# Mamba-2 scan with a cosine-gated feed-forward: B and C of seven pairs of sequences loaded in 32-token blocks and transposed by VectorE

## The chip, the cores and the metric

The kernel runs on one core of a Trainium2 chip. The metric is the device time of one execution in microseconds (us). A profiled execution has a span that is a little shorter than the timed one (377.9 us against 379.95 us for the same run), since the span leaves out what lies before the first and after the last instruction. Times inside the kernel are given from the span's start.

## The reference

Two blocks follow each other. The first is a selective state-space scan over `x` (4 sequences, 8 heads, 768 tokens, 32 channels) with a decay `a` per token and head, and `B` and `C` with a state of 16 per token and head. With `cum` the running sum of `log a` inside a chunk, each chunk computes

```
CB      = C_i . B_j                       (over the 16 of the state)
y_intra = (CB * exp(cum_i - cum_j), j <= i) x
y_inter = (C_i . state) * exp(cum_i)
state   = exp(cum_last) * state + sum_j B_j x_j exp(cum_last - cum_j)
y       = y_intra + y_inter
```

The result is brought to 3072 rows (sequence and token) of 256 (head and channel). The second block is `h = y w_in` (256 to 2048), `g = h * cos(h)`, `out = g w_out` (2048 to 256). All is float32.

## The kernel before

The tokens are cut into six chunks of 128 (`NC = 6`), each with four sequences (`b` = 0 to 3). Sequences go in two pairs, `u = 0` and `u = 1`, so there are twelve pairs (chunk, pair). The feed-forward is cut into 16 pieces of 128 of its 2048 columns per chunk (`NF = 16`), and the whole kernel is one loop over 96 such steps `n` plus two (`LAG = 2`). Chunk `c` owns the steps 16c to 16c + 15. The order is written out by hand (`tc.manual_schedule()`): every engine executes its instructions in the order of the program, and a small table, `plan`, says at which steps the scan of chunk c is worked on beside the feed-forward of chunk c - 1.

A step of the feed-forward has a chain over four engines. TensorE multiplies `y` by a piece of `w_in` into a PSUM bank `hp` (L519). ScalarE takes the integer number of turns `k` (L523), VectorE the remainder `w` (L525), ScalarE its sine (L530), VectorE the product `gT` of `hp` and the cosine (L535), GpSimd four differences `gd` for a seven-product form of the second matrix product (L560 to L563). TensorE multiplies them by `w_out` two steps later into `o` (L616; L578 in the first chunk). There are two `hp` banks, so `hp` of step n + 2 has to wait for `gT` of step n.

The scan of a pair takes four stations. Decays (`lam`, L345) come from running products on VectorE. At the step before the pair's turn, `reaches` (L336) makes the running products of `a` along the tokens, on VectorE. At its turn, `turn2` brings B and C from "token on the partition" to "head and state on the partition": four transposes of 128x128 on TensorE through PSUM (`tp`, L406), then `bT` (a copy, L409) and `cT` (two scaled copies, L412) on ScalarE, and `rT = tp * reach` (L414) on VectorE. One step later `intra2` multiplies them (`g`, L423), and `masked` (L436) applies the decays on VectorE. At the end of the pair, or of both pairs of a chunk, `finish2` computes `y` (L450, L457), copies it to `yT`, forms the new sums `s_ps` (L478, which read `x` and the scaled B) and carries the state.

In chunks 2 to 5 the first pair turns at step 16(c - 1) + 7, the second at 16(c - 1) + 11, and both finish at 16(c - 1) + 14. Chunk 1 differs: its first pair turns at step 11 and finishes at 14, its second turns at step 18 and finishes at step 21.

All loads and most stores are issued by SyncE (SP), whose queue is in program order too. A transfer that has to wait, for a buffer or for its data, holds up all behind it. Transfers also take turns on eight semaphores, so each waits for the transfer eight places before it to land. `load` (L119) brings a chunk's B and C (tile `bc`) and x (tile `xr`), with a token on each partition; a load of B for four sequences has 4096 rows of 64 bytes. Chunk c + 2 is loaded at step 16c. These tiles come from a pool with three buffers. `load_a` (L127, `arow`) and `load_along` (L137) fetch the decays for the next chunk, `along` with its 8 heads spread over 128 partitions.

The lines below fix the places of the work, chunk by chunk: the step at which a chunk's plan starts, its pairs' turns, the halves of the decays, and its end.

```
late = [((0,), {0: 11}, [...], 14),
        ((1,), {1: NF + 2}, [...], NF + 5)]
at_once = (0, 1), {0: 7, 1: 11}, 14
```

Of the kernel before, what the change touches and what calls it, by code (L numbers as in the profile page):

```python
# [8 lines left out]
FP32 = mybir.dt.float32  # L9
# [16 lines left out]
def kernel(  # L26
# [29 lines left out]
    nc = tc.nc  # L56
    V, ACT, G, PE = nc.vector, nc.scalar, nc.gpsimd, nc.tensor

    NB, H, S, D = x.shape
    N = B.shape[-1]  # L60
    P = 128
    NC = S // P
    DM, DF = moe_w_in.shape
    KT = DM // P
    NF = DF // P
# [5 lines left out]
    W = P // 2  # L71

    const = ctx.enter_context(tc.tile_pool(name="const", bufs=1))
    loads = ctx.enter_context(tc.tile_pool(name="loads", bufs=3))
    rows = ctx.enter_context(tc.tile_pool(name="rows", bufs=NB))
    scan = ctx.enter_context(tc.tile_pool(name="scan", bufs=2))
    states = ctx.enter_context(tc.tile_pool(name="states", bufs=3))
# [11 lines left out]
    def pair(name):  # L89

        return psum.tile([P, 2, 4 * P], FP32, tag="scan", bufs=2, name=name)


    raw, arow, along = {}, {}, {}
    ones = const.tile([P, P], FP32, name="ones")
    V.memset(ones, 1.0)

# [10 lines left out]
    def load(c, seqs=(0, NB)):  # L108

        if c >= NC:  # L110
            return
        if c not in raw:
            raw[c] = (loads.tile([P, 2, NB * H, N], FP32, tag="bc", name="bc"),
                      loads.tile([P, NB, H, D], FP32, tag="xr", name="xr"))
        bc, xr = raw[c]
        xr = xr.rearrange("p b h d -> p (b h) d")
        rs = slice(seqs[0] * H, seqs[1] * H)
        for dst, src in ((bc[:, 0, rs], B), (bc[:, 1, rs], C), (xr[:, rs], x)):
            nc.sync.dma_start(out=dst, in_=src[seqs[0]:seqs[1], :, c * P:(c + 1) * P, :]  # L119
                              .rearrange("b h s n -> s (b h) n"))  # L120

    def load_a(c, seqs=range(NB)):
        if c >= NC:
            return
        for b in seqs:
            arow[c, b] = t = rows.tile([P, H, P], FP32, tag="arow", name="arow")
            nc.sync.dma_start(  # L127
                out=t, in_=a_cut[b, :, c * P:(c + 1) * P].unsqueeze(0).to_broadcast([P, H, P]))

    def load_along(c, seqs=range(NB)):  # L130

        if c >= NC:
            return
        if c not in along:
            along[c] = rows.tile([P, NB, P], FP32, tag="along", bufs=2, name="along")
        for b in seqs:
            nc.sync.dma_start(  # L137
                out=along[c][:, b], in_=a_all[b, :, c * P:(c + 1) * P].unsqueeze(1)
                .to_broadcast([H, N, P]))
# [20 lines left out]
    def fetch(which, i, eng=nc.sync):  # L160
        src = (moe_w_in[:, i * WC:(i + 1) * WC].rearrange("(k p) f -> p k f", p=P)
               if which == "in" else
               moe_w_out[i * WF * P:(i + 1) * WF * P, :].rearrange("(f p) m -> p f m", p=P))
        if src.dtype == FP32:
            eng.dma_start(out=kept(which, i), in_=src)
            return
        words[which, i] = t = conv.tile([P, 2 * WC, 2], U32, tag="words", bufs=8, name="words")
        eng.dma_start(  # L168
            out=t.rearrange("p (k f) w -> p k (f w)", k=src.shape[1]), in_=src.bitcast(U32))
# [49 lines left out]
    for b in range(NB):  # L219
# [4 lines left out]
        out=a_in, in_=a.rearrange("(u b) h (c p) -> (b h c) u p", u=NU, p=P))  # L224
# [4 lines left out]
    ident = const.tile([P, P], FP32, name="ident")  # L229
# [59 lines left out]
    def heads(b):  # L289
        return slice(b * H, (b + 1) * H)  # L290
# [106 lines left out]

    def turn2(c, u):  # L400
        bc = raw[c][0]

        tp = pair("tp")[:, 0].rearrange("p (s k i) -> p s k i", s=2, k=2)
        for s in range(2):
            for k in range(2):
                PE.transpose(tp[:, s, k],  # L406
                             bc[:, k, heads(2 * u + s)].rearrange("p h n -> p (h n)"), ident)
        bT = scan.tile([P, 2, P], FP32, tag="bT2", bufs=1, name="bT2")
        ACT.copy(out=bT, in_=tp[:, :, 0])  # L409
        cT = scan.tile([P, 2, 2, P], FP32, tag="cT2", bufs=1, name="cT2")  # L410
        for t in range(2):
            ACT.activation(cT[:, :, t], tp[:, :, 1], AF.Copy, scale=slot[:, t:t + 1])  # L412
        rT = scan.tile([P, 2, P], FP32, tag="rT", name="rT")
        V.tensor_tensor(out=rT, in0=tp[:, :, 1], in1=reach[c, u], op=ALU.mult)  # L414
        part[c, u] = [bT, cT, rT]
# [93 lines left out]
    def first(n):  # L509
        c, f = divmod(n, NF)  # L510
        hp[n] = bank([P, TB], "hp", "h")

        u, j = turn_of(n)
        to_ = hp[n].rearrange("p (e t s i) -> p e t s i", e=2, t=2, s=2)
        y = yT[c].rearrange("p k (u s t i) -> p k u t s i", u=2, s=2, t=2)
        for e in range(2):
            fs = slice((2 * j + e) * P, (2 * j + e + 1) * P)
            for k in range(KT):
                PE.matmul(to_[:, e], lhsT=w_in[:, k, fs], rhs=y[:, k, u],  # L519
                          start=(k == 0), stop=(k == KT - 1), skip_group_check=True)  # L520

        k = ffn.tile([P, TB], I32, tag="k", name="k")
        ACT.activation(k, hp[n], AF.Copy, bias=0.25, scale=INV_2PI)  # L523
        turns[n] = w = ffn.tile([P, TB], FP32, tag="w", name="w")
        V.scalar_tensor_tensor(out=w, in0=hp[n], scalar=INV_2PI, in1=k,  # L525
                               op0=ALU.mult, op1=ALU.subtract)

    def gate(n):
        cos = turns[n]
        ACT.activation(cos, cos, AF.Sin, bias=quarter, scale=TWO_PI)  # L530
# [165 lines left out]
    for dst, src in ((a_cut, cut), (a_all, la)):  # L696
        nc.sync.dma_start(
            out=dst.rearrange("(u b) h (c p) -> (b h c) u p", u=NU, p=P), in_=src)
# [27 lines left out]
    def first_scan():  # L726

        finish(3, "o")
        for u in range(2):
            sums[u] = pair("s_ps")[:, :, 0:2 * D]  # L730
            for t in range(2):
                sum_up(0, 2 * u + t, sums[u][:, t])

    def chunk1(b):
        load(1, (b, b + 1))
        load_along(1, (b,))
        load_a(1, (b,))

    def rest_of_loads():
        for w in (("out", 2), 0, ("in", 4), ("out", 3), ("in", 5), ("out", 4), 1,  # L740
                  ("in", 6), ("out", 5), ("in", 7), 2, ("out", 6), ("out", 7), 3):
            chunk1(w) if isinstance(w, int) else fetch(*w)
        load(2)

    def pairs(n):

        return [(c, u) for c, at, _, turn_at, _, _ in plan for u in turn_at
                if at + turn_at[u] == n]
# [4 lines left out]
    def halved(c, b, t):  # L753
        decays(c, b, t)
        if t == 1:
            load_a(c + 1, (b,))

    def ends(n):
        return [(c, us) for c, at, us, _, _, end in plan if at + end == n]

    rest_of_loads()
    for n in range(NC * NF + LAG):
        c, f = divmod(n, NF)
        if n < NC * NF:
            if f == 0 and c > 0:
                load(c + 2)
            first(n)
            if n == 0:
                first_scan()
            for at in pairs(n):  # L770
                turn2(*at)
            rests = [rest] if n == 0 else []
            if n + 1 in piece:
                rests.append(grade(*piece[n + 1], later=True))
            gate(n)
            for rest in rests:
                if rest:
                    rest()
            if n in piece and n > 1:
                join(*piece[n])  # L780

            behind = [lambda at=at: halved(*at) for at in halves_at(n)]
            behind = [lambda at=(c, 2 * u + 1): masked(*at) for c, u in pairs(n - 2)] + behind
            if n not in piece and behind:
                behind.pop(0)()
            gated(n)
            if n < 2:
                join(*piece[n])
            for do in (*behind, *unsummed):
                do()  # L790
            unsummed.clear()
            if n in (1, 2):
                carry(0, n - 1, sums[n - 1])
        for i, js in differ_at.get(n, ()):
            differ_w(i, js)
        if n >= LAG:
            second(n - LAG)
        for c, u in pairs(n - 1):
            intra2(c, u)
            masked(c, 2 * u)  # L800
        for c, us in ends(n):
            finish2(c, us)
            if 1 in us:
                raw.pop(c)
        for c, u in pairs(n + 1):
            for b in (2 * u, 2 * u + 1):
                reaches(c, b)
                load_along(c + 1, (b,))


# [28 lines left out]
```

## Time and profile before

| what | value |
|---|---|
| time, median of three runs (lowest, highest) | 380.73 us (380.5, 380.94) |
| span of the profiled execution | 377.9 us |
| TensorE busy (matmul) | 372.2 us, 98% |
| VectorE busy | 274.4 us, 73% |
| GpSimd busy | 214.3 us, 57% |
| ScalarE busy | 177.1 us, 47% |
| DMA, mean over the span | 80 GB/s, packets 39.6% of 16 engines' time on the main queue |
| TensorE's four transposes per pair (L406) | 40 instructions for ten pairs, 273 ns listed for each |

In the profile, PE is TensorE's matmul, PEld its weight load, DVE is VectorE, ACT ScalarE, POOL GpSimd, and SPq the queue of SyncE. A listed duration of a matmul covers its whole way through the array, and matmuls overlap; what one costs is read from the distance between starts. A float32 matmul shows as two records, a transpose as one. The chain of waits follows the work that ended last back in time; what is on it sets the span.

### The profile page before, as it was taken

How to read it: one execution, taken by the hardware profiler on the slowest of the kernel's cores; microseconds unless marked ns; L12 is line 12 of the kernel's file. 1: busy time of each engine (PE TensorE's matmuls, PEld its weight loads, DVE VectorE, ACT ScalarE, POOL GpSimd, SP SyncE). 2: the span in 40 equal slices, each digit the busy share in tenths (PEclk: the TensorE clock that was granted, in tenths of full speed). 3: DMA queues.
4: the chain of work that ended last, by engine and by line, in shares of the span. 5: the costliest groups of instructions: out<-in, count | busy, mean ns of one | idle time of the engine just before them, and what ended most of it. 6: DMA issues, size and time to landing. Idle time of an engine off the chain costs nothing.

```text
span 377.9 us, 7680 instructions
## 1 busy us (share of the span) xinstructions
PE 372.2 (98%) x2980; PEld 329.6 (87%) x2980; DVE 274.4 (73%) x422; ACT 177.1 (47%) x312; POOL 214.3 (57%) x330
## 2 busy tenths in 40 slices
PE   8999999999999999999999999999999999999996
PEld 2578888889989899998999998899998989999995
DVE  8879999899688747966747985756886762454543
ACT  3887756444435434444434354424444533543442
POOL 6767565579865437673544683443685343454551
PEclk9999999999999999999999999999999999999999
DMA  6989979979230971420681340100010000010011
GB/s 82 234 255 293 255 206 131 182 98 175 78 102 26 148 63 57 135 76 2 82 73 57 83 122 7 42 2 2 1 30 3 10 19 2 0 29 0 2 28 28
DMA packets 106370, 30.41 MB, mean 80 GB/s; under 512 B 75520, under 2 KB 102240, under 8 KB 106336
## 3 DMA queue, kind: packets, MB, share of 16 engines
q1 hardware_dynamic: 106176, 29.81, 39.6%
q8 instruction: 23, 0.38, 0.5%
q10 hardware_dynamic: 160, 0.13, 0.1%
q14 instruction: 11, 0.09, 0.1%
HBM read 26.59 MB, written 3.34 MB: 79 GB/s over the span
## 4 chain that ended last, share of the span: by engine, by line
PE 92%; SPq 3%; DMA 1%; ACT 1%; issue 0%; DVE 0%; POOL 0%; POOLq 0%
PE hp L519 43%; PE o L616 33%; PE o L578 7%; PE g L423 3%; SPq L119 3%; PE y L457 3%; DMA words<-in_moe_w_out_dram 1%; PE y L450 1%; PE tp L406 1%; PE o L661 1%; PE s_ps L478 0%; ACT mag L193 0%; POOL w_out L217 0%; SPq L168 0%; DVE mag L209 0%
## 5 line engine op out<-in xcount | busy, mean ns | idle before, releaser
L519 PE MATMUL hp<-yT,w_in 128*128 128x256 f32 x768 | 183.8, 382 | 0.4 <-POOL w_in L217 0.3
L519 PEld LDWEIGHTS hp<-yT,w_in 128*128 128x128 f32 x768 | 139.4, 190 | 21.2 <-issue 2.9
L560 POOL TENSOR_TENSOR gd<-gT 128x256 f32<-128x256 f32 x79 | 59.8, 757 | 103.6 <-DVE gT L535 79.2
L530 ACT ACTIVATE w<-w,quarter 128x512 f32<-128x512 f32 x96 | 69.3, 722 | 79.3 <-DVE w L525 79.3
L525 DVE SCALAR_TENSOR_TENSOR w<-hp,k 128x512 f32<-128x512 f32 x96 | 65.7, 684 | 54.5 <-ACT k L523 54.3
L523 ACT ACTIVATE k<-hp 128x512 int32<-128x512 f32 x96 | 57.1, 595 | 95.7 <-PE hp L519 95.5
L535 DVE TENSOR_TENSOR gT<-hp,w 128x512 f32<-128x512 f32 x96 | 65.1, 678 | 32.3 <-ACT w L530 27.1
L616 PE MATMUL o<-words,gd 128*128 128x128 f32 x474 | 65.8, 275 | 0.0
L616 PEld LDWEIGHTS o<-words,gd 128*128 128x128 f32 x474 | 59.3, 192 | 0.0
L345 DVE TENSOR_TENSOR_SCAN lam<-arow,unit 128x512 f32<-128x512 f32 x40 | 56.3, 1406 | 0.0
L563 POOL TENSOR_TENSOR gd<-gT,gd 128x128 f32<-128x128 f32 x79 | 47.3, 599 | 6.2
L616 PEld LDWEIGHTS o<-w_out,gT 128*128 128x128 f32 x316 | 46.9, 191 | 3.6
L616 PE MATMUL o<-w_out,gT 128*128 128x128 f32 x316 | 48.0, 274 | 0.0
L562 POOL TENSOR_TENSOR gd<-gT,gd 128x128 f32<-128x128 f32 x79 | 42.4, 537 | 6.2
L578 PE MATMUL o<-w_out,gT 128*128 128x256 f32 x128 | 30.3, 380 | 0.4 <-POOL w_out L217 0.4
L616 PE MATMUL o<-words,gT 128*128 128x128 f32 x158 | 30.6, 275 | 0.0
L616 PE MATMUL o<-w_out,gd 128*128 128x128 f32 x158 | 30.6, 275 | 0.0
L578 PEld LDWEIGHTS o<-w_out,gT 128*128 128x128 f32 x128 | 24.2, 190 | 4.0 <-POOL w_out L217 0.8
L436 DVE TENSOR_TENSOR m<-g,lam 128x512 f32<-128x512 f32 x40 | 25.5, 679 | 0.0
L616 PEld LDWEIGHTS o<-words,gT 128*128 128x128 f32 x158 | 24.0, 192 | 0.0
L616 PEld LDWEIGHTS o<-w_out,gd 128*128 128x128 f32 x158 | 24.0, 192 | 0.0
L633 DVE TENSOR_TENSOR sum<-ps,sum 128x256 f32<-128x256 f32 (+1 forms) x27 | 16.7, 645 | 0.6
(91 smaller groups left out, 280.7 us busy)
## 6 DMA issues: line engine op xcount, KB each, us to landing
arow<-a_cut SPq DMA_DIRECT2D x20, 512.0 KB, 4.1
words<-in_moe_w_in_dram SPq DMA_DIRECT2D x8, 512.0 KB, 6.3
words<-in_moe_w_out_dram SPq DMA_DIRECT2D x8, 512.0 KB, 8.4
out_dram<-sum SPq DMA_DIRECT2D x18, 128.0 KB, 2.5
xr<-in_x_dram SPq DMA_DIRECT2D x4, 512.0 KB
along<-a_all SPq DMA_DIRECT2D x20, 64.0 KB
xr<-in_x_dram SPq DMA_DIRECT2D x8, 128.0 KB
bc<-in_B_dram SPq DMA_DIRECT2D x4, 256.0 KB, 5.0
```

The lines of the kernel that those rows point to most:

```text
L345: V.tensor_tensor_scan(out=lam[c, b][:, hs].rearrange("p h i -> p (h i)"), data0=rows_.rearrange("p h i -> p (h i)"), data1=unit.rearrange ...
L436: V.tensor_tensor(out=of[0], in0=g[q][:, :, s * 2 * P:(s + 1) * 2 * P], in1=of[1], op=ALU.mult)
L519: PE.matmul(to_[:, e], lhsT=w_in[:, k, fs], rhs=y[:, k, u], start=(k == 0), stop=(k == KT - 1), skip_group_check=True)
L523: ACT.activation(k, hp[n], AF.Copy, bias=0.25, scale=INV_2PI)
L525: V.scalar_tensor_tensor(out=w, in0=hp[n], scalar=INV_2PI, in1=k, op0=ALU.mult, op1=ALU.subtract)
L530: ACT.activation(cos, cos, AF.Sin, bias=quarter, scale=TWO_PI)
L535: V.tensor_tensor(out=gT[n], in0=hp.pop(n), in1=cos, op=ALU.mult)
L560: G.tensor_tensor(out=d[:, 0:2], in0=g[:, 1:2].to_broadcast([P, 2, P]), in1=g[:, 3::-3], op=ALU.subtract)
L562: G.tensor_tensor(out=d[:, 2], in0=g[:, 0], in1=d[:, 0], op=ALU.subtract)
L563: G.tensor_tensor(out=d[:, 3], in0=g[:, 2], in1=d[:, 2], op=ALU.subtract)
L578: PE.matmul(o[c, u][:, t], lhsT=g[:, 2 * e + t], rhs=w_out[:, 2 * j + e], start=(j == e == t == 0), stop=(j == NJ - 1 and e == 1), skip_gr ...
L616: PE.matmul(at[q], lhsT=a_[q], rhs=w[q], start=(j == 0 and q in starts), stop=(j == NJ - 1), skip_group_check=True)
```

## The change

For the pairs from chunk 2's second on (seven of twelve), B and C are fetched a second way: in blocks of 32 tokens, so that each partition holds, for one of four heads and one of 32 tokens, the 16 values of the state. A transpose of 32x32 squares on VectorE then gives the layout that four TensorE transposes gave. The aim is to take these transposes, and the copy `bT` behind them, off TensorE and ScalarE.

Per pair this needs 32 transfers (2 sequences, B and C, 4 blocks of tokens, 2 sets of heads) of 128 rows of 64 bytes each. They are issued by SP, four at the end of each of eight steps that start at step 16(c - 1) - 9 + 8u: steps 15 to 22 for chunk 2's second pair, 23 to 30 and 31 to 38 for the pairs of chunk 3, and so on. VectorE's two transposes stand behind `reaches`, at the end of the step before the pair's turn, that is at steps 26, 38, 42, 54, 58, 70 and 74. The block tile takes two buffers, the transposed tile one, which `bT` of the other pairs shares. To make room, the tiles `bc` and `xr` have two buffers instead of three. B is still loaded by tokens for the sums of the state; C of chunks 3, 4 and 5 no longer is.

```diff
-    loads = ctx.enter_context(tc.tile_pool(name="loads", bufs=3))
+    loads = ctx.enter_context(tc.tile_pool(name="loads", bufs=2))
...
-        for dst, src in ((bc[:, 0, rs], B), (bc[:, 1, rs], C), (xr[:, rs], x)):
+        for dst, src in ((bc[:, 0, rs], B), (bc[:, 1, rs], C), (xr[:, rs], x))[::2 if c > 2 else 1]:
             nc.sync.dma_start(out=dst, in_=src[seqs[0]:seqs[1], :, c * P:(c + 1) * P, :]
                               .rearrange("b h s n -> s (b h) n"))
+
+    def by_blocks(c, u):
+        return (c, u) >= (2, 1)
+
+    def load_blocks(c, u):
...
+        blocks[c, u] = to_ = loads.tile([P, 2, 2, 4, 2, N], FP32, tag="blocks", name="blocks")
+        for s in range(2):
+            for k, src in enumerate((B, C)):
+                of = src[2 * u + s, :, c * P:(c + 1) * P].rearrange(
+                    "(q h) (m t) n -> m h q t n", h=2, t=32)
+                for m in range(4):
+                    for h in range(2):
+                        nc.sync.dma_start(out=to_[:, k, s, m, h], in_=of[m, h])
+                        yield
...
+    def turn_blocks(c, u):
+        turned[c, u] = t = scan.tile([P, 2, 2, P], FP32, tag="turned", bufs=1, name="turned")
+        for k in range(2):
+            V.transpose(out=t[:, k].rearrange("p s i -> p (s i)"),
+                        in_=blocks[c, u][:, k].rearrange("p s m h n -> p (s m h n)"))
+        del blocks[c, u]
+
     def turn2(c, u):
         bc = raw[c][0]
...
+        if by_blocks(c, u):
+            tp = turned.pop((c, u)).rearrange("p k s i -> p s k i")
+            bT = tp[:, :, 0]
+        else:
...
+    block_loads = {NF * (c - 1) - 9 + 8 * u: (c, u) for c in range(2, NC) for u in range(2)
+                   if by_blocks(c, u)}
...
             for b in (2 * u, 2 * u + 1):
                 reaches(c, b)
                 load_along(c + 1, (b,))
+            if by_blocks(c, u):
+                turn_blocks(c, u)
+        for at, (c, u) in block_loads.items():
+            if at == n:
+                loading = load_blocks(c, u)
+            if at <= n < at + 8:
+                for _ in range(4):
+                    next(loading)
```

More of the change, by code (lines that the diff above doesn't have):

```diff
@@ L91, in pair @@
         return psum.tile([P, 2, 4 * P], FP32, tag="scan", bufs=2, name=name)
-    raw, arow, along = {}, {}, {}
+    raw, arow, along, blocks = {}, {}, {}, {}
     ones = const.tile([P, P], FP32, name="ones")
@@ L395, in finish @@
         ACT.copy(out=yT[0][:, :, b * P:(b + 1) * P], in_=y[:, 0:2])
+    turned = {}
+    def turn_blocks(c, u):
[4 more added lines that the diff above has]
+        del blocks[c, u]
     def turn2(c, u):
         bc = raw[c][0]
[L403 to L409, printed above, removed]
+        if by_blocks(c, u):
+            tp = turned.pop((c, u)).rearrange("p k s i -> p s k i")
+            bT = tp[:, :, 0]
+        else:
+            tp = pair("tp")[:, 0].rearrange("p (s k i) -> p s k i", s=2, k=2)
+            for s in range(2):
+                for k in range(2):
+                    PE.transpose(tp[:, s, k],
+                                 bc[:, k, heads(2 * u + s)].rearrange("p h n -> p (h n)"), ident)
+            bT = scan.tile([P, 2, 2, P], FP32, tag="turned", bufs=1, name="bT2")[:, 0]
+            ACT.copy(out=bT, in_=tp[:, :, 0])
         cT = scan.tile([P, 2, 2, P], FP32, tag="cT2", bufs=1, name="cT2")
```

## The prediction

> **What bounds the kernel now.** First the page's busy shares and the chain of waits, to see which engine sets the end.
>
> ```profile
> PE 372.2 (98%) x2980; PEld 329.6 (87%) x2980; DVE 274.4 (73%) x422; ACT 177.1 (47%) x312; POOL 214.3 (57%) x330
> ...
> PE 92%; SPq 3%; DMA 1%; ACT 1%; issue 0%; DVE 0%; POOL 0%; POOLq 0%
> ```
>
> TensorE does. From about 25 us on its matmuls follow each other without a gap, so an instruction taken off TensorE shortens the span by its issue time, and a wait put into it lengthens the span by as much. Next the chain in order of time, around one group of four transposes (columns: start, length, what).
>
> ```profile
> 159.44 1.73 PE hp L519 x8
> 161.16 1.56 PE o L616 x14
> 162.73 1.73 PE hp L519 x8
> 164.89 1.56 PE o L616 x14
> ```
>
> Without transposes `o` starts 1.72 us after `hp`; with them 2.16. Four transposes cost TensorE 0.44 us, not four times the 273 ns that one is listed with: they are pipelined.
>
> Then the queue of SyncE, which issues all loads. First the timeline of SP at the start of chunk 1, where chunk 3 is loaded, and the durations of two kinds of transfer from their tiles' views (min/median/max, ns):
>
> ```profile
> 78.81 0.52 SPq L119 DMA_DIRECT2D bc<-in_B_dram  x1
> 79.78 3.07 SPq L119 DMA_DIRECT2D bc<-in_C_dram  x1
> 82.96 3.08 SPq L119 DMA_DIRECT2D xr<-in_x_dram  x1
> 86.14 4.04 SPq L586 DMA_DIRECT2D out_dram<-ob  x2
> 90.27 0.55 SPq L127 DMA_DIRECT2D arow<-a_cut  x1
> 90.91 2.21 SPq L586 DMA_DIRECT2D out_dram<-ob  x2
> 93.18 1.29 SPq L137 DMA_DIRECT2D along<-a_all  x2
> ```
> ```profile
> L137 SPq DMA_DIRECT2D along<-a_all x20: 577/619/812, 26.2 to 242.9; - x20
> L127 SPq DMA_DIRECT2D arow<-a_cut x20: 360/367/2727, 27.1 to 223.4; - x20
> ```
>
> The reader is to see that a transfer holds SP for 0.4 to 0.65 us however small it is, and that the transfer behind a 4096-row load waits some 3 us more. Last the timelines of TensorE and VectorE at the first pair that changes (chunk 2, second pair, step 27), and the chain two steps on:
>
> ```profile
> 99.22 0.41 PE L478 MATMUL s_ps<-xr,sc 128*32 128x64 f32 x16
> ```
> ```profile
> 121.73 0.73 DVE L336 TENSOR_TENSOR_SCAN reach<-along,ones 128x128 f32<-128x128 f32 x2
> 122.38 0.66 DVE L525 SCALAR_TENSOR_TENSOR w<-hp,k 128x512 f32<-128x512 f32 x1
> 122.96 0.41 DVE L414 TENSOR_TENSOR rT<-tp,reach 128x256 f32<-128x256 f32 x1
> 123.29 1.21 DVE L345 TENSOR_TENSOR_SCAN lam<-arow,unit 128x512 f32<-128x512 f32 x1
> 124.42 0.66 DVE L535 TENSOR_TENSOR gT<-hp,w 128x512 f32<-128x512 f32 x1
> ```
> ```profile
> 126.07 1.92 PE hp L519 x8
> ```
>
> The `s_ps` line is the last read of chunk 1's `xr`, at 99.6 us. The last line is `hp` of step 29, which needs the PSUM bank that step 27's `gT` (ended 125.1) sets free: 1.0 us of slack.
>
> **What the Trainium skill says.** "Vector Engine (DVE) Microarchitecture Reference", section 3.8, has the 32x32 transpose run at one element per cycle and lane; no trace here shows one yet. "DMA: Bandwidth & Descriptors", "Why a DMA increments its semaphore by 16 and not by 1", lets a transfer run on the largest number of engines up to 16 that divides the outer dimension of both sides: an estimate of 4 engines for a block (its source has 4 heads outermost) and 8 for `along`. The trace doesn't show the split. "TensorE: Matmul & The Clock Gate", Part 1, says that an idle stretch of about 3.4 us halves TensorE's clock and that it takes about 3.4 us of work to come back. The granted clock here is 0.998 throughout, and no such idle stretch occurs, so this trace doesn't test it.
>
> **The change, part by part.**
>
> TensorE loses 7 x 4 transposes: 7 x 0.44 = 3.1 us, all on the path.
>
> ScalarE loses seven `bT` copies (367 ns each), and two `cT` copies per pair read SBUF. ScalarE is 47% busy and waits for `hp`: nothing.
>
> VectorE gains two transposes of 128x256 per pair. No row shows one; bounds are the 0.41 us of `rT`, also 256 elements per lane, and twice that. I take 0.42. `rT` now reads two SBUF operands and no longer waits for TensorE: even. For the first pair of a chunk, step 39's `gT` ended at 167.6 and `hp` of step 41 began at 170.8: 0.84 us fit. For the second pair the slack is less (step 43's `gT` ended 184.0, `hp` of step 45 began 185.7, and the transposes taken out bring that to 185.2): 0.84 just fit. Nothing here, at 0.42 each; some tenths at more.
>
> DMA engines: 224 transfers of 128 rows of 64 bytes more, three loads of C fewer. From 100 us on the page has these engines half busy or less in all but four of its slices: hidden.
>
> SP's queue is where it goes wrong. Step 16 issues chunk 3's loads. With three buffers `xr` took the place of chunk 0's. With two it takes that of chunk 1, whose second pair ends only in step 21, at 99.6 us. In the built program this transfer waits for that last `s_ps` matmul, and SP runs in order: from about 86 to 99.6 us it stands still, with 28 of the 32 block transfers of chunk 2's second pair behind it, which step 27 needs. (Only here: in later chunks the old tiles are read out two steps before the load.)
>
> What does one block transfer hold SP for? `along` is nearest: same 128 rows, a source of three dimensions against a destination of two. 0.619 and a gap of 0.045, or 1.29 for two, is about 0.665 us. The low bound is `arow`, 0.41 with its gap. I take 0.665. From 99.6, in program order:
> - `xr` 0.6, two `ob` stores held up behind it as at 86.14, with a gap 4.1: 104.3
> - 4 blocks 2.7, `arow` 0.45, two stores 1.4, two `along` 1.3: 110.1
> - 8 blocks 5.3, `arow` 0.45, 12 blocks 8.0: 123.9
> - `arow` and two `along` 1.75, 4 blocks 2.7: 128.3; landing 2.0 (the quickest store): 130.3.
>
> VectorE would reach the second transpose at about 122.9. So it stands for over 7 us, with `w`, `rT`, `lam` and `gT` of step 27 queued behind it. From `w` to the end of `gT` was 2.7 us: 130.3 + 0.4 + 2.7 = 133.4, and with 0.1 for the signal `hp` of step 29 starts at 133.5. Without its transposes it would start at 126.07 - 0.44 = 125.6. Stall 7.9 us. `g` of step 28 waits for the same tile and lies inside it.
>
> TensorE then idles some 7 us in one piece, so by the clock page I add an estimate of 3.4 us at half speed, 1.7 us lost; the bounds are 0 and 3.4.
>
> For the later pairs the same sum leaves room. 64 blocks per chunk are 43 us of SP, the loads with their hold-ups 7, stores, `along` and `arow` 7: 57 of a chunk's 59.6 us. They arrive, with little to spare.
>
> Sum: -3.1 + 7.9 + 1.7 = +6.5. 380.7 + 6.5 = 387.2 us.
>
> **The rivals.**
> - B, blocks are cheap to issue. At 0.41 us the 28 transfers end 28 x 0.255 = 7.1 us earlier, the stall is 0.8 and the clock stays: -3.1 + 0.8, 378.4 us, faster. For it: `arow` has more rows and takes 0.37. Against: `along` resembles it more, stores of 128 rows also take 0.64, and each transfer waits for the one eight before it to land, which with `arow` (4.1 us to land) costs about a microsecond twice at this pace.
> - C, SP saturates. At 0.75 per block 64 take 48 us and a chunk needs 62 of its 59.6; second pairs of chunks 3 and 4 come about 3 us late each as well. The stall at step 27 grows to 10.3: -3.1 + 10.3 + 6.5 + 1.7 = +15.4, 396 us. Against: only the maximum of `along`, 812 ns, is that long.
> - D, no lateness, but VectorE is the bound: transposes of 0.8 us overrun the second pairs' slack by some 0.6 us four times. -3.1 + 2.4: 380.0, no change to speak of. Against: needs both a cheap issue and a slow transpose.
>
> **How the numbers follow.** Stall at step 27: 0.78; B 0.12; C 0.06; D 0.04. Within the first, 0.55 per block takes 3.2 us off (384.0), 0.48 takes off 5.2 and the clock loss too (380.3), and 0.70 with twice the clock loss adds 2.7 (390); 393 leaves 3 us for landing and hold-ups. The range 380.5 to 393 leaves out B and C, 0.18. Faster: B and half of D, 0.14. Same: half of D and the low edge, 0.04. Slower: 0.82.
>
> **What would show it.** SP's timeline: chunk 3's `xr` issued at about 99.6 instead of 83, and blocks at 0.6 to 0.7 us apiece. VectorE's waits: the second transpose of the first pair waits for a transfer of `blocks` until about 130. TensorE: one idle stretch of about 7 us near 124 to 132, a dip of the granted clock after it, and no gap elsewhere; chain steps with 1.72 us from `hp` to `o` at the seven pairs. I am wrong if blocks issue in under 0.47 us, if no gap stands at step 28, or if gaps recur in each chunk.

## The result and the profile after

The changed kernel takes 384.68 us (median of four runs, 383.6 to 385.17) where the kernel before took 380.62 beside it: a ratio of 1.0105, with a 95% interval of 1.0079 to 1.0132. It is 4.1 us slower. The prediction was 387.2 us, in a range of 380.5 to 393.

The page first: busy shares, the chain of waits, and the two rows of slices in which the change is seen (each digit is the busy share, or the granted TensorE clock, of a fortieth of the span).

```profile
span 381.8 us, 7915 instructions
...
PE 371.9 (97%) x2952; PEld 328.6 (86%) x2952; DVE 278.5 (73%) x436; ACT 176.2 (46%) x305; POOL 213.7 (56%) x330
...
PE   8999999999999599999999999999999999999996
...
PEclk9999999999999699999999999999999999999999
...
PE 93%; DVE 3%; POOL 1%; SPq 1%; DMA 1%; issue 1%; ACT 0%; DVEq 0%; POOLq 0%; ACTq 0%
```

TensorE is still what sets the end, and its row has one hole, in the slice from 124 to 134 us. The clock dips in the same slice and nowhere else. A cause that comes back in each chunk would have made four or seven holes.

The timeline of SP shows what stands before it (start, length in us, what).

```profile
79.38 2.39 SPq L137 DMA_DIRECT2D blocks<-in_B_dram  x4
85.61 0.38 SPq L119 DMA_DIRECT2D bc<-in_B_dram  x1
99.90 0.37 SPq L119 DMA_DIRECT2D xr<-in_x_dram  x1
100.37 3.33 SPq L617 DMA_DIRECT2D out_dram<-ob  x2
103.75 2.37 SPq L137 DMA_DIRECT2D blocks<-in_B_dram  x4
...
109.50 4.67 SPq L137 DMA_DIRECT2D blocks<-in_C_dram  x8
114.27 0.42 SPq L145 DMA_DIRECT2D arow<-a_cut  x1
114.74 4.63 SPq L137 DMA_DIRECT2D blocks<-in_B_dram  x8
119.42 2.28 SPq L137 DMA_DIRECT2D blocks<-in_C_dram  x4
121.79 0.42 SPq L145 DMA_DIRECT2D arow<-a_cut  x1
122.26 1.25 SPq L155 DMA_DIRECT2D along<-a_all  x2
123.55 2.32 SPq L137 DMA_DIRECT2D blocks<-in_C_dram  x4
```

Chunk 3's `xr` was issued at 82.96 us before and is now issued at 99.90; between 86 and 99.9 SP issues nothing. (It had stood from 81.8 to 85.6 as well, until chunk 1's last transposes on TensorE had read the old `bc` tile.) The queue then runs on without a pause, the blocks at about 0.58 us each (2.32 for four), and the last of this pair are issued at 125.9, some 3 us after VectorE gets to them. VectorE's timeline at that place:

```profile
121.95 0.73 DVE L354 TENSOR_TENSOR_SCAN reach<-along,ones 128x128 f32<-128x128 f32 x2
122.60 0.41 DVE L423 STREAM_TRANSPOSE turned<-blocks 128x256 f32<-128x256 f32 x1
127.36 0.45 DVE L423 STREAM_TRANSPOSE turned<-blocks 128x256 f32<-128x256 f32 x1 [4.34 <-DMA blocks<-in_C_dram]
127.72 0.65 DVE L556 SCALAR_TENSOR_TENSOR w<-hp,k 128x512 f32<-128x512 f32 x1
128.30 0.40 DVE L445 TENSOR_TENSOR rT<-turned,reach 128x256 f32<-128x256 f32 x1
128.63 1.21 DVE L363 TENSOR_TENSOR_SCAN lam<-arow,unit 128x512 f32<-128x512 f32 x1
129.75 0.66 DVE L566 TENSOR_TENSOR gT<-hp,w 128x512 f32<-128x512 f32 x1
```

The transpose of B runs, that of C waits 4.34 us for its blocks, and `gT` of step 27, which ended at 125.1 before, ends at 130.4. TensorE's timeline then reads:

```profile
128.80 2.09 PE L454 MATMUL g<-cT,turned 32*128 32x256 f32 x16 [4.02 <-ACT cT L443]
130.82 3.73 PE L550 MATMUL hp<-yT,w_in 128*128 128x256 f32 x8
134.39 0.61 PE L647 MATMUL o<-w_out,gT 128*128 128x128 f32 x4
```

`hp` takes 3.73 us here where it takes 1.89 elsewhere. The table by stretches gives the reason; its columns are the stretch, its length, busy time of PE, PEld, DVE, ACT and POOL with counts, the granted clock, the DMA share and GB/s.

```profile
121.00:124.70 3.70, 3.70 (x27) 3.38 (x25) 2.01 (x5) 0.00 (x0) 0.80 (x2) 1.00 0.52 143
124.70:128.80 4.10, 0.08 (x2) 0.00 (x1) 1.45 (x4) 0.96 (x3) 0.00 (x0) 0.85 0.30 55
128.80:132.00 3.20, 3.20 (x19) 2.22 (x20) 2.34 (x4) 1.76 (x3) 1.69 (x4) 0.50 0.68 175
132.00:134.40 2.40, 2.40 (x8) 1.86 (x7) 1.76 (x3) 0.00 (x0) 1.88 (x4) 0.51 0.16 15
134.40:138.00 3.60, 3.60 (x26) 3.39 (x25) 2.48 (x4) 1.38 (x3) 0.20 (x2) 1.00 0.47 112
```

After the idle stretch TensorE works at half its clock until 134.4. The 0.85 in the idle stretch is a mean: in finer stretches of the trace the clock falls from 1.00 to 0.50 at 127.54. The account from the chain: `hp` of step 29 begins at 130.89. In the kernel before it began at 126.07, and the step ahead of it began 0.22 us later there than here, so the delay is 130.89 - (126.07 - 0.22) = 5.0 us. From `hp` to `o` it then takes 3.66 us instead of 1.93: 1.7 us more. Less 7 x 0.44 = 3.1 us of transposes this makes 3.7 before rounding. The spans differ by 3.9; the 0.2 us between stand ahead of all this, since `hp` of step 27 already starts 0.22 us later here (118.03 against 117.81).

### The profile page after: what moved, and what is told of

Read it like the earlier page. It is cut to its first block, busy times and chain, and to the rows that moved or that the text cites. A ratio compares the mean times of both kernels' runs of the same rounds, so it can differ in the third digit from the quotient of the medians.

```text
span 381.8 us, 7915 instructions
## 1 busy us (share of the span) xinstructions
PE 371.9 (97%) x2952; PEld 328.6 (86%) x2952; DVE 278.5 (73%) x436; ACT 176.2 (46%) x305; POOL 213.7 (56%) x330
## 4 chain that ended last, share of the span: by engine, by line
PE 93%; DVE 3%; POOL 1%; SPq 1%; DMA 1%; issue 1%; ACT 0%; DVEq 0%; POOLq 0%; ACTq 0%
PE hp L550 42%; PE o L647 31%; PE o L609 7%; PE g L454 3%; PE y L488 3%; PE y L481 1%; PE warm L101 1%; PE a_ps L317 1%; DVE mag L227 1%; PE g L392 1%; POOL w_in L235 1%; DMA blocks<-in_C_dram 1%; PE o L692 0%; PE s_ps L509 0%; DVE sum L664 0%
## 5 line engine op out<-in xcount | busy, mean ns | idle before, releaser
L346 POOL TENSOR_TENSOR sc<-bc,lam 128x128 f32<-128x128 f32 x20 | 8.3, 417 | 16.7 <-DVE lam L363 9.4
```

## The experiments

**Chunk 3's load later.** All blocks of chunk 2's second pair but four then stand ahead of the load, and the load finds chunk 1's tile already free.

```diff
-            if f == 0 and c > 0:
+            if f == (6 if c == 1 else 0) and c > 0:
                 load(c + 2)
```

> The changed kernel with chunk 3's load moved from step 16 to step 22, behind the end of chunk 1; nothing else. Theory (the stop of SP's queue on chunk 1's x tile, and the clock loss that follows, are the whole cost): no transfer of blocks comes late, no idle stretch at step 28, and only the 3.1 us of the transposes taken off TensorE remain: about 377.5 us against 380.6 of the kernel before, ratio 0.992. Rival (VectorE or the 224 small transfers cost by themselves): 380 us or more.

Measured: 377.24 us, ratio 0.9914 (0.990 to 0.9929). The stop and what follows it were the whole loss: with one load moved by six steps the change is a gain of 3.3 us (2.7 to 3.8), and the prediction had 3.1 for the transposes. SP's timeline of this run shows no gap before these blocks are out, and the load among the blocks:

```profile
94.73 4.67 SPq L137 DMA_DIRECT2D blocks<-in_B_dram  x8
99.45 2.28 SPq L137 DMA_DIRECT2D blocks<-in_C_dram  x4
101.83 0.41 SPq L119 DMA_DIRECT2D bc<-in_B_dram  x1
102.34 3.59 SPq L119 DMA_DIRECT2D xr<-in_x_dram  x1
...
110.25 2.44 SPq L137 DMA_DIRECT2D blocks<-in_C_dram  x4
```

The last four blocks are out at 112.7, some ten microseconds before VectorE asks for them.

**The transposes put back.** The kernel with the later load, with four transposes of its row-wise B per changed pair; nobody reads their result.

```diff
+            spare = pair("tp")[:, 0].rearrange("p (s i) -> p s i", s=4)
+            for s in range(4):
+                PE.transpose(spare[:, s], bc[:, 0, heads(s)].rearrange("p h n -> p (h n)"), ident)
```

> As the kernel with the later load, with four TensorE transposes put back per changed pair; their result is not used. Theory (a group of four costs TensorE 0.44 us): 3.1 us more than without them, so 380.6 us, ratio 1.000 to the kernel before. Rival (what was gained is the PSUM bank and ScalarE's copy, not TensorE's time): as fast as without them, 377.5.

Measured: 380.73 us, ratio 1.000 (0.9991 to 1.0008). All of the gain comes with the transposes: 3.5 us for 28 of them, 0.5 us for four, by the difference of the two medians, against 0.44 read from the chain. ScalarE's copy `bT` stays out here, so it was not the gain. The transposes also take their PSUM bank again, but no wait of TensorE for it shows in this run, and at step 27 its chain has `o` 2.17 us after `hp` instead of 1.73: it is TensorE's time.

**Two buffers and nothing else**, in the kernel before.

```diff
-    loads = ctx.enter_context(tc.tile_pool(name="loads", bufs=3))
+    loads = ctx.enter_context(tc.tile_pool(name="loads", bufs=2))
```

> The kernel before with two buffers in place of three for the loads, and nothing else. SP stops at chunk 3's x until about 99.6 us here too, but behind it stand only stores and decays that are needed at 114 us or later. Theory (the stop costs only with the 28 transfers behind it): 380.6 us, no change. Rival (the lost buffer costs by itself): 382 to 385.

Measured: 380.2 us, ratio 0.9997 (0.9987 to 1.0006). SP stops here as well, for 6.7 us ahead of `bc` and for 11.7 us ahead of `xr`:

```profile
78.61 0.36 SPq L127 DMA_DIRECT2D arow<-a_cut  x1
85.65 0.37 SPq L119 DMA_DIRECT2D bc<-in_B_dram  x1
86.08 2.13 SPq L119 DMA_DIRECT2D bc<-in_C_dram  x1
99.95 0.37 SPq L119 DMA_DIRECT2D xr<-in_x_dram  x1
100.41 3.33 SPq L586 DMA_DIRECT2D out_dram<-ob  x2
103.84 0.55 SPq L127 DMA_DIRECT2D arow<-a_cut  x1
```

Two stops of together 18 us cost nothing by themselves. A stop costs when 28 transfers that are needed soon stand behind it.

**Fewer and more blocks behind the stop.** Two kernels: the blocks of this pair begun at step 14, and the first four held back until step 16.

```diff
+    block_loads[14] = block_loads.pop(15)
```
```diff
-                for _ in range(4):
+                for _ in range(0 if n == 15 else 8 if n == 16 else 4):
```

> The changed kernel with the block transfers of chunk 2's second pair begun at step 14 instead of 15: 8 ahead of the stop of SP's queue, 24 behind. Theory (each transfer behind the stop delays step 27 by its issue time, 0.58 us): the stall of 5.0 us shrinks by 4 x 0.58 = 2.3 to 2.7 us, the idle stretch is under 2 us and the clock stays: 380.6 - 3.1 + 2.7 = 380.2 us. If the clock drops all the same: 382. Rival (the stall comes from landing, not from the count of issues): 384.7.

> The changed kernel with the first four block transfers of chunk 2's second pair moved behind the stop: none ahead, 32 behind. Theory: 2.3 us more stall, the same clock loss: 387.0 us. Rival (as for the earlier start): 384.7. If the clock loss grows with the idle stretch: 388.

Measured: 378.04 us (ratio 0.9933, 0.9919 to 0.9948) and 386.47 us (1.0156, 1.0138 to 1.0174). The second came out as expected within its interval. The first was expected at 380.2: the direction was right and the size was not. Starting a step earlier also ends a step earlier, and so the last blocks moved ahead of an `arow` and two `along` transfers as well, 1.76 us of SP that the expectation had left standing in front of them. 4 x 0.58 + 1.76 = 4.1 us by the count; in the trace the last blocks are out at 121.99 us instead of 125.87, and the second transpose starts at 123.82 instead of 127.36, 3.9 and 3.5 us sooner (this run is itself 0.2 us behind at step 27). Both runs show that the position in the queue, counted in issue times, sets when step 27 goes on. They also bracket the clock. TensorE's waits in the first are too short to change it:

```profile
125.26 1.15 PE L454 MATMUL g<-cT,turned 32*128 32x256 f32 x16 [0.28 <-ACT cT L443]
127.03 1.97 PE L550 MATMUL hp<-yT,w_in 128*128 128x256 f32 x8 [0.63 <-DVE gT L566]
```

In the second, 6.92 us of idle time are followed by 6.3 us of work at half clock, where 4.02 us were followed by 5.6 (`hp` is 3.78 us long instead of 3.73).

**The idle stretch filled.** In the changed kernel, four matmuls of ones into the bank that `g` then overwrites.

```diff
         g = [pair("g") for _ in range(2)]
+        if (c, u) == (2, 1):
+            fill(g[0][:, 0].rearrange("p (k i) -> p k i", k=4), 4)
```

> The changed kernel with four matmuls of ones (128x512) ahead of the scores g of chunk 2's second pair, in the idle stretch; their result is overwritten. Theory (TensorE's clock drops because of the idle stretch, and that costs 1.8 us beyond the stop): g and the next hp run at full clock, hp of step 29 still starts where it did but takes 1.9 in place of 3.7 us, 382.9 us against 384.7. Rival (hp is slow there because it waits for data): 384.7 or, if the added matmuls delay g, more.

Measured: 382.0 us, ratio 1.0044 (1.0028 to 1.0059), against 1.0105. By the two ratios that is 2.3 us less, give or take 1.2, where 1.8 was expected. TensorE's timeline:

```profile
125.02 3.60 PE L101 MATMUL g<-ones 128*128 128x512 f32 x8
129.24 1.15 PE L456 MATMUL g<-cT,turned 32*128 32x256 f32 x16 [0.62 <-ACT cT L443]
131.01 1.97 PE L552 MATMUL hp<-yT,w_in 128*128 128x256 f32 x8 [0.63 <-DVE gT L568]
```

`hp` starts within 0.2 us of where it did, at 131.0, and runs at full clock. So the delay by the late blocks and the loss of clock are two costs, and matmuls that compute nothing take the second away.

**VectorE's transposes twice**, on the kernel with the later load.

```diff
-        for k in range(2):
+        for k in (0, 0, 1, 1):
             V.transpose(out=t[:, k].rearrange("p s i -> p (s i)"),
```

> The kernel with the later load, each VectorE transpose executed twice. Theory of the prediction (the slack of the second pairs is some 0.24 us after the first two transposes): 0.82 us more of VectorE per pair cost about 0.6 us at each of four second pairs, nothing at the first pairs: 379.6 us against 377.2. Rival (VectorE has room everywhere): 377.2.

Measured: 381.15 us, ratio 1.0016 (1.0008 to 1.0023). That is 3.9 us more than with single transposes, not 2.4. TensorE's waits at a second pair, in step 44 and 45:

```profile
185.17 1.15 PE L454 MATMUL g<-cT,turned 32*128 32x256 f32 x16 [0.36 <-ACT cT L443]
186.67 1.97 PE L550 MATMUL hp<-yT,w_in 128*128 128x256 f32 x8 [0.35 <-DVE gT L566]
```

The expectation looked at `gT` and `hp` alone. `g` now waits as well, for the scaled copies `cT`, which ScalarE can't start before the transpose is done. In the whole run `hp` waits 2.0 us for `gT` and `g` 1.6 us for `cT`. With single transposes it was 0.3 and nothing, so some 0.8 us are added at each of four second pairs. The doubling itself adds more than the 0.82 us that were taken for it. From the first transpose to `w` behind the last, VectorE's timelines have 1.62 us here and 0.67 with single transposes:

```profile
182.48 1.70 DVE L423 STREAM_TRANSPOSE turned<-blocks 128x256 f32<-128x256 f32 x4
184.10 0.65 DVE L556 SCALAR_TENSOR_TENSOR w<-hp,k 128x512 f32<-128x512 f32 x1
```
```profile
181.20 0.74 DVE L423 STREAM_TRANSPOSE turned<-blocks 128x256 f32<-128x256 f32 x2
181.87 0.65 DVE L556 SCALAR_TENSOR_TENSOR w<-hp,k 128x512 f32<-128x512 f32 x1
```

That is 0.95 us per pair, and four times 0.95 is 3.8 of the 3.9 us: next to nothing is absorbed. The single transposes used up the slack.

**Twice, and a step earlier.** VectorE's sums of the output stand in the step in which a second pair's transposes are made; a step earlier there is idle time.

```diff
+        for c, u in pairs(n + 2):
+            if by_blocks(c, u):
+                turn_blocks(c, u)
         for c, u in pairs(n + 1):
...
-            if by_blocks(c, u):
-                turn_blocks(c, u)
```

> The later load, each transpose twice, and all transposes one step earlier. If it is the place behind the sums that has no slack, the second 0.82 us per pair fit into VectorE's idle time of the step before: 377.2 us, as with single transposes. Rival (VectorE's total time is the bound there): 381, as with the doubled transposes in the old place.

Measured: 377.89 us, ratio 0.9925 (0.9912 to 0.9937). The doubled transposes now fit. It is the place that has no room, not VectorE.

**Eight pairs**, with the later load: chunk 2's first pair too.

```diff
-        return (c, u) >= (2, 1)
+        return (c, u) >= (2, 0)
```

> As the kernel with the later load, and chunk 2's first pair by blocks too (eight pairs; C of chunk 2 no longer loaded by tokens). Its 32 transfers are issued after about 66 us and needed at step 22, about 105 us. Theory: they arrive, and 0.44 us more is gained: 377.1 us. Rival (they queue behind the first loads and come late, or they hold up chunk 2's decays): 378 or more.

Measured: 376.86 us, ratio 0.9902 (0.9887 to 0.9917). The blocks arrive. The interval overlaps that of seven pairs, so the 0.44 us of the eighth pair is not shown by the times.

**Eight pairs, transposes a step earlier**, first with the load of chunk 3 at step 22, then at step 23.

> The eight-pair kernel with VectorE's transposes one step earlier, so that in the second pairs they no longer stand behind the sums of the output. If the second pairs have no slack left (the doubled transposes say so), a few tenths of us come back: 376.4 us, ratio 0.989. Rival (the transposes already fit): 376.9, no difference to the eight pairs.

> The eight pairs with the earlier transposes, with chunk 3's load at step 23 instead of 22, behind the last four blocks of chunk 2's second pair. In the run with the load at step 22 VectorE waited 2.5 us for those four. Theory: that wait goes and the earlier transposes cost nothing: 376.5 us, ratio 0.989. Rival (the earlier place itself is bad, in other pairs as well): 379 or more.

Measured: 381.33 us (ratio 1.002, 1.0008 to 1.0032) and 377.43 us (0.9908, 0.9891 to 0.9926). The first was a miss of the same kind as the change itself. The load of chunk 3 stands ahead of the last four blocks, and its hold-ups made them late for a transpose that now comes a step sooner:

```profile
117.15 0.43 DVE L423 STREAM_TRANSPOSE turned<-blocks 128x256 f32<-128x256 f32 x1
120.09 0.45 DVE L423 STREAM_TRANSPOSE turned<-blocks 128x256 f32<-128x256 f32 x1 [2.50 <-DMA blocks<-in_C_dram]
```

With the load one step later the time is back at that of the eight pairs. The profile with the load at step 22 is of one of that kernel's quickest executions (379.58 us of 379.34 to 383.93), so the other two microseconds of its median are not seen in it. The clock measured with each execution gives a hint. In sixteen of the 22 its mean was 0.996 or less, and these took 381.0 us or more; in the other six, the profiled one among them, it was 0.999 or 1.0, and four of these took under 380.6. One period of 3.41 us at half clock (the last section has these periods) makes a mean of 0.996 over 380 us. So the late blocks may well have cost most executions the clock too; as no trace of such an execution is kept, this is not shown.

## Why the prediction was right

1. TensorE as the bound, 0.44 us for four transposes: right. The gain is 3.3 us with the load moved, and vanishes when the transposes are put back.
2. The place of the stop, in SP's queue at chunk 3's `xr`, because two buffers make it wait for chunk 1's last `s_ps`: right, 99.9 us against 99.6. Moving the load removes it.
3. A block's issue: the term that was mis-sized. It was taken as 0.665 us from `along`; the row of the kernel after has a median of 536 ns, 0.58 with the gap, so 28 of them end 2.4 us sooner. Some of the rest of the queue was shorter too (`xr` and the two stores 3.8 us from 99.9, not 4.7). The last blocks were there at 127.4 instead of 130.3.
4. The stall: 5.0 us instead of 7.9, by the terms of point 3. The path from the blocks to `hp` was nearly right. By way of `gT` it gives 127.4 + 0.45 + 2.7 = 130.5, and `gT` did end at 130.4, but `hp` began at 130.8: what it waited for last was `g`, which took 2.09 us at half clock instead of 1.08. The prediction had `g` hidden inside the stall. About 0.3 us of the 5.0 therefore belong to the clock.
5. The clock: 1.7 us predicted, and `hp` to `o` took 1.7 us longer; that the two agree is partly luck. The prediction took 3.4 us at half speed. TensorE worked at half speed for 5.6 us, of which `g`, whose loss lay mostly inside the wait for `gT`, had 2.0. "TensorE: Matmul & The Clock Gate", Part 1 of the Trainium skill, speaks of about 3.4 us of idleness. Here the clock fell at 127.54, 2.8 us after the last matmul had ended at 124.78 by the profile (3.0 us in the kernel with no blocks ahead), sooner than the page's figure; waits of 0.28 and 0.63 us, or a filled stretch, did not lower it. It stayed halved for 5.6 us after work came back, longer than the page's 3.4. From fall to rise it is 6.83 us, and 10.24 in the kernel with no blocks ahead: two and three times 3.41. Counting such periods from the fall, the clock rose in both at the end of the first that had work in it from end to end (130.96 to 134.37 us, and 134.84 to 138.26). Whether the matmuls of `g`, on 32 rows, count for as much as the others was not tried.
6. VectorE's transposes: 0.41 us, as taken. That agrees with the one element per cycle and lane of "Vector Engine (DVE) Microarchitecture Reference", section 3.8, in so far as `rT` takes as long for as many elements. The view that they "just fit" at second pairs was right, with less to spare than thought.
7. No gap in later chunks: right; SP did not saturate.

The sum in its place: -3.1 + 5.0 + 1.7 = 3.6, or 3.9 with the rounding and the 0.2 us from before step 27, where the prediction had 6.5; the times say 4.1. The prediction's own line for 0.55 us per block, 384.0, is closer than its middle. One slip in it: rival D's 380.0 us lies outside the range too, so the range leaves out more than the 0.18 that it counts.

## What to carry to other kernels

A buffer taken away is paid for where the next load waits, and the price is set by what stands behind that load in the same in-order queue: look there, and count issue times up to the first transfer that someone needs soon. Before giving a change up, move the waiting load behind what it holds up; here one line turned a loss of 4 us into a gain of 3. Where work is moved to an engine with idle time, what counts is the idle time at that place in its order, not its share of the span.

## What was not expected of the hardware

A transfer of 128 rows of 64 bytes held SP for 536 ns (least 528), less than the 619 ns of `along` with as many rows of 512 bytes, and more than the 367 ns of `arow` with 1024 rows. The number of rows doesn't order them.

The granted clock changes on a grid. In the trace of the changed kernel it is halved for 6.83 us, then full for 245.76 us up to the last microseconds; in that of the kernel with no blocks ahead it is halved for 10.24 us. These are 2, 72 and 3 times 3.413 us. So an idle stretch that lowers the clock is paid for in whole periods, and the part that falls on work depends on where in a period the work comes back.

The prediction said that the trace doesn't show over how many DMA engines a transfer is split. The landing signals recorded in the trace do: after one early signal a block's landing gives 4 and that of `along` 8, while `arow` gives 16 and no early one. The estimate of 4 and 8 was right.
